# When batch 3's x is loaded, and where batch 2's scores stand, in a fused cross-attention and gated feed-forward kernel

## The chip, the cores and the metric

The kernel runs on one core of a Trainium2 chip. The core has a matrix engine (TensorE, PE in the profile), a vector engine (VectorE, DVE), a scalar engine (ScalarE, ACT), a general engine (GpSimd, POOL) and a synchronising engine (SyncE, SP), which here only issues transfers. Each engine runs its own list of instructions in order. Transfers are carried by 16 DMA engines, which all queues share. The metric is the device time of the launch in microseconds (us); lower is better. Four runs of the kernel before took 228.4 to 231.78 us, median 230.49.

## The reference

There are B = 8 batches with H = 8 heads, S = 512 tokens, Ns = 32 state rows and D = 64 values a head. For each batch and head the tokens read the state by a softmax over the 32 state rows, and the state rows read the tokens by a softmax over the 512 tokens. Both results stand one after the other and go through a gated feed-forward layer.

```python
scores  = scale * x @ state.T;   a  = softmax(scores);  xread = a  @ state
scores2 = scale * state @ x.T;   a2 = softmax(scores2); sread = a2 @ x
y   = concatenate([xread, sread], axis=2)        # B, H, S + Ns, D
t   = y.transpose(0, 2, 1, 3).reshape(B * (S + Ns), H * D)
out = (sigmoid(t @ w_gate) * (t @ w_val)) @ w_out     # 512 -> 1536 -> 512
```

## The kernel before

**Tiling.** A batch's 512 tokens are four chunks of 128 (index `c`), its eight heads two halves of four (index `i`), the 1536 hidden columns twelve groups of 128 (index `f`, NF = 12). Arithmetic on TensorE is in bf16.

**A batch's stages.** `load_x` (L70) brings x from memory in fp32 as one transfer of 1 MB; the caller names the queue, SP or GpSimd. `cast_x` (L100) makes it bf16 (`xb`). `at_xT_dma` (L125) has SP issue four DMA transposes, one a chunk, which give `xT`. `S_mm` (L130) computes the scores of one half of the heads with eight matmuls; every group of four matmuls needs all four chunks of `xT`. `S_exp` (L136, ScalarE) makes E; `n_sum` (L150) and `n_mul` (L171, VectorE) make the normalised `ab`; `aT_dma` (L194) has SP issue four DMA transposes of it, which give `aT`. `at_Eb` (L142, GpSimd) makes a bf16 copy of E, which the matmuls of the state read (`sr_mm`, L203) use.

**Feed-forward.** The state is multiplied into the gate and value weights first (`sw_mm`, L234; `sw_wide`, L257, is half of a batch's share), which gives `SW`. `gv_mm` (L282) multiplies `SW` by `aT`, four matmuls a group; `gv_th` (ScalarE) and `gv_glu` (VectorE) make the gated product; `out_mm` (L312) multiplies a third of the groups of one chunk by `wo`, four matmuls a call, and every third call finishes a chunk, which ScalarE scales and SP writes out.

**Order.** No scheduler: the order of the source is the order on every engine. Batches 0 and 1 have a start-up written out by hand (L393 to L582), which does all their gate/value work. Then a loop over b from 1 to 8 and over f from 0 to 11 (L584) interleaves the output of batch b - 1, the gate/value work of batch b and the attention of batch b + 1 (`nb`). For b = 1 there is no gate/value work left, and f = 0, 1, 2 only call `out_mm` for batch 0; the scores of batch 2 follow the second of these calls. The state weights of batch 2 (`sw_wide`) come at f = 3 and 6, its state read at f = 9, its first gate/value group at b = 2, f = 0, and the scores of batch 3 at b = 2, f = 1 and 2.

**Around the change.** On GpSimd's queue the transfers of the start-up stand in this order: the last weight loads, x of batch 2 (L504), three loads of `wo` (L505 to L507, 512 KB each), x of batch 3 (L508). GpSimd then pads a state tile (L576) and casts x of batch 2 and of batch 3 as each lands. SP issues the four transposes of batch 2's `xT`, the four of batch 3's, then the four of batch 2's `aT`, then the output writes. The tiles `xb`, `xT`, `aT`, `ab` and E have two buffers each, x in fp32 has three, the output tiles have four. `gate` (L85) is a one-element copy on GpSimd whose only purpose is that GpSimd's queue waits until its argument has landed; it is used in the start-up already:

```python
    def gate(landed):
        nc.gpsimd.tensor_copy(pre[:, 1:2], landed)
```

Of the kernel before, what the change touches and what calls it, by code (L numbers as in the profile page):

```python
# [16 lines left out]
def kernel(  # L17
# [14 lines left out]
    nc = tc.nc  # L32
# [31 lines left out]
    AT, OU, GV, SWP = (p_at, "at"), (p_out, "outp"), (p_gv, "gv"), (p_sw, "swp")  # L64
    xfs, xbs, xTs = {}, {}, {}
# [4 lines left out]
    def load_x(b, eng, parts=1, hold=None):  # L70
        xf = stg.tile((128, H, 4, D), FP, name="xf")
        if hold is not None:

            hold.memset(xf[:, 0, 0, 0:1], 0.0)
        v = x[b].rearrange("h (p c) d -> p h c d", c=4)
        n = H // parts
        for i in range(parts):
            eng.dma_start(xf[:, n * i:n * i + n], v[:, n * i:n * i + n])
        xfs[b] = xf
# [5 lines left out]
    def gate(landed):  # L85

        nc.gpsimd.tensor_copy(pre[:, 1:2], landed)
# [8 lines left out]
    def load_wo(q):  # L96
        nc.gpsimd.dma_start(wo[:, 4 * q:4 * q + 4],
                            moe_w_out.rearrange("(k p) n -> p k n", p=128)[:, 4 * q:4 * q + 4])

    def cast_x(b, cp, lo, n):  # L100
        if b not in xbs:
            xbs[b] = xp.tile((128, 4, H, D), BF, name="xb")
        cp(xbs[b].rearrange("p c h d -> p h c d")[:, lo:lo + n], xfs[b][:, lo:lo + n])  # L103


    def xT_tile(b):
        if b not in xTs:
            xTs[b] = ap_.tile((128, 4, 4, 128), BF, name="xT")
        return xTs[b]
# [15 lines left out]
    def at_xT_dma(b):  # L125
        xT = xT_tile(b)
        for c in range(4):
            nc.sync.dma_start_transpose(xT[:, :, c], xbs[b][:, c].rearrange("p h d -> p (h d)"))  # L128

    def S_mm(b, i, place):  # L130
        ps = held["S", b, i] = place[0].tile((128, 4, 2, 2, Ns), FP, name="Sp", tag=place[1])
        for jj in range(2):
            for c in range(4):
                nc.tensor.matmul(ps[:, c, :, jj], xTs[b][:, 2 * i + jj, c], sTz[:, b, 2 * i + jj], start=True, stop=True)  # L134

    def S_exp(b, i):  # L136
        if b not in E1s:
            E1s[b] = ap_.tile((128, 4, 2, 4, Ns), FP, name="E1")
        nc.scalar.activation(E1s[b][:, :, :, 2 * i:2 * i + 2].rearrange("p c e j n -> p (c e) j n"),  # L139
                             held["S", b, i].rearrange("p c e j n -> p (c e) j n"), AF.Exp, scale=scale)  # L140
# [6 lines left out]
    def halfE(b, i):  # L147
        return E1s[b][:, :, :, 2 * i:2 * i + 2].rearrange("p c e j n -> p (c e) j n")

    def n_sum(b, i):  # L150
        rs = ap_.tile((128, 8, 2), FP, name="rs")
        nc.vector.tensor_reduce(rs, halfE(b, i), AX.X, ALU.add)  # L152
        ri = held["ri", b, i] = ap_.tile((128, 8, 2), FP, name="ri")
        nc.vector.reciprocal(ri, rs)
# [16 lines left out]
    def n_mul(b, i, eng):  # L171
        if b not in abs_:
            abs_[b] = ap_.tile((128, 4, 2, 128), BF, name="ab")
        ri = held["ri", b, i]
        eng.tensor_tensor(abs_[b].rearrange("p c e (j n) -> p (c e) j n", n=Ns)[:, :, 2 * i:2 * i + 2], halfE(b, i),  # L175
                          ri.unsqueeze(3).to_broadcast((128, 8, 2, Ns)), ALU.mult)
# [7 lines left out]
    def aT_tile(b):  # L184
        if b not in aTs:
            aTs[b] = ap_.tile((128, 4, 2, 128), BF, name="aT")
        return aTs[b]
# [6 lines left out]
    def aT_dma(b):  # L194
        for c in range(4):
            nc.sync.dma_start_transpose(aT_tile(b)[:, c], abs_[b][:, c].rearrange("p e k -> p (e k)"))  # L196
# [60 lines left out]
    def sw_wide(b, v):  # L257

        if b not in SWs:
            SWs[b] = fp.tile((128, 2, 2, dff), BF, name="SW", bufs=2)  # L260
        lo = 768 * v
        for k, places in enumerate(((OU, AT), (SWP, SWP), (SWP, SWP))):
            pss = [p[0].tile((128, 512), FP, name="swp", tag=p[1]) for p in places]
            if k < 2:
                sw_mm(pss, b, k, lo, 512, 0)
            else:
                for w in range(2):
                    sw_mm(pss, b, w, lo + 512, 256, 256 * w)
            for e in range(2):
                if k < 2:  # L270
                    sw_left[b, v, k, e] = (SWs[b][:, e, k, lo:lo + 512], pss[e])
                else:
                    sw_left[b, v, k, e] = (SWs[b][:, e, :, lo + 512:lo + 768], pss[e].rearrange("p (w n) -> p w n", w=2))

    def sw_cp(b, lo, w, e, cp):
        cp(*sw_left.pop((b, lo, w, e)))  # L276
# [5 lines left out]
    def gv_mm(b, f, place):  # L282
        n = n_of(b)
        fs = slice(f * 128, (f + 1) * 128)
        pss = []
        for w in range(2):
            ps = place[0].tile((128, 512), FP, name="gvp", tag=place[1])[:, :n]
            if b < B:
                for g in range(2):
                    nc.tensor.matmul(ps, SWs[b][:, g, w, fs], aTs[b][:, :, g], start=(g == 0), stop=(g == 1))  # L290
            else:
                for j in range(4):
                    nc.tensor.matmul(ps, (wg, wv)[w][:, j, fs], XS[:, j], start=(j == 0), stop=(j == 3))  # L293
            pss.append(ps)
        held["gv", b, f] = pss
# [209 lines left out]
    load_wo(0)  # L505
    load_wo(1)
    load_wo(2)  # L507
    load_x(3, nc.gpsimd)  # L508
    sw_cp(1, 512, 0, 1, act)
    gv_mm(0, 6, SWP)  # L510
    gv_glu(1, 1)
# [64 lines left out]
    pad(2, 6)  # L576
    cast_x(2, pool, 0, 4)
    cast_x(2, pool, 4, 4)
    cast_x(3, pool, 0, 4)
    cast_x(3, pool, 4, 4)  # L580
    at_xT_dma(2)
    at_xT_dma(3)  # L582

    for b in range(1, B + 1):  # L584
        nb = b + 1 if b + 1 < B else None
        for f in range(NF):

            v, q = divmod(f, 6) if b > 1 else (0, f - 3) if f < 6 else (1, f - 6)
            if nb is not None and q == 0:
                sw_wide(nb, v)  # L590
                sw_cp(nb, v, 0, 0, act)
                sw_cp(nb, v, 0, 1, act)
            ahead = nb is not None and q == 0
            for first in (ahead, not ahead):
                if first and b > 1:
                    gv_mm(b, f, SWP if b == B and f % 2 else GV)
                    gv_th(b, f)
                    gv_glu(b, f)
                elif not first and (b < B or f < 9):
                    out_mm(b - 1, f)  # L600
            if nb is not None:
                if q == 0:
                    sw_cp(nb, v, 1, 0, vec)
                if b == 1 and f == 1:
                    for i in range(2):
                        S_mm(nb, i, (AT, OU)[i])
                        S_exp(nb, i)
                        n_sum(nb, i)
                        n_mul(nb, i, nc.vector)
                    aT_dma(nb)  # L610
                for k in ({1: (3,), 3: (4,), 4: (5,)} if b > 1 else {0: (3,), 1: (4, 5)}).get(q, ()):
                    sw_cp(nb, v, k // 2, k % 2, act)
                g = f
                if g in (1, 2) and b > 1:
                    S_mm(nb, g - 1, AT)
                    S_exp(nb, g - 1)
                if f in (6, 7):
                    n_tok(nb, f - 6)
                    if f == 7:
                        n_split(nb, 0)  # L620
                elif f == 8:
                    n_split(nb, 1)
                elif f == 9:
                    sr_mm(nb, AT)
                    sr_inv(nb)
                    if b == 1:
                        sr_fin(nb)
                elif f == 10 and b > 1:
                    sr_fin(nb)
                if g in (2, 4) and b > 1:  # L630
                    n_sum(nb, g // 2 - 1)
                elif g in (3, 5) and b > 1:
                    n_mul(nb, g // 2 - 1, nc.vector)
                if g == 3:
                    at_Eb(nb)
                if nb + 2 < B and f == (6 if b == 1 else 3):
                    load_x(nb + 2, nc.sync)
                if g == 5 and b > 1:
                    aT_dma(nb)
                if f == 5 and b > 1:  # L640
                    if nb + 1 < B:
                        cast_x(nb + 1, pool, 0, 4)
                        cast_x(nb + 1, pool, 4, 4)
                        at_xT_dma(nb + 1)
# [33 lines left out]
```

## Time and profile before

| What | Value |
|---|---|
| median of four runs | 230.49 us |
| lowest and highest | 228.4 and 231.78 us |
| the profiled execution's own time | 230.5 us |
| its span, first to last instruction | 228.7 us |
| granted TensorE clock | 1.000 |
| bytes moved by DMA | 27.57 MB |
| transposes `xT`: issues, median issue to landing | 24, 2.5 us |
| transposes `aT`: issues, median issue to landing | 24, 2.4 us |
| loads of x from SP, 1 MB: median issue to landing | 7.0 us |
| loads of x from GpSimd, 1 MB (batches 2 and 3): median | 14.6 us |
| loads of `wo` from GpSimd, 512 KB: median | 12.6 us |

Times in the profile are microseconds from the first instruction. A row of the chain or of a timeline gives the start, the length, the engine with the line of the source, and what is written from what is read; "q" after an engine's name is its sequencer, which issues transfers; a trailing bracket gives the idle time before the row and what ended it. The row of slices shows forty equal parts of the span, 5.7 us each, with the busy share in tenths. q0 is the queue of the transfers that GpSimd issues, q1 the one of those that SP issues.

### The profile page before, as it was taken

Reading aid. Unit: us, or ns where it says so; the run is one execution under the profiler, and the core shown is the slowest. Engines: PE = TensorE matmul, PEld = TensorE weight load, DVE = VectorE, ACT = ScalarE, POOL = GpSimd, SP = SyncE. Lnnn points to the kernel's source line nnn. Section 1 sums busy time; section 2 is a strip of 40 time slices with the busy share of each in tenths; the row PEclk is TensorE's granted clock in tenths of the full one; section 3 lists DMA queues with packets and bytes.
Section 4 is the critical chain, followed back from the end, with each engine's and each line's share of the span. In section 5 each row is a group of like instructions: output and inputs, shape, how many; then the busy total and the mean of one; then the engine's idle time right before and its main releaser. Section 6 shows DMA issues by size and latency. Waiting matters only on the chain.

```text
span 228.7 us, 4786 instructions
## 1 busy us (share of the span) xinstructions
PE 218.1 (95%) x1855; PEld 113.1 (49%) x1880; DVE 139.9 (61%) x233; ACT 130.7 (57%) x244; POOL 46.0 (20%) x90
## 2 busy tenths in 40 slices
PE   7779999979999999999999999999999999999994
PEld 6655345434444445444444544454445444466744
DVE  2489899838358854886488747874687443332311
ACT  3569787548458476756675567556755544422411
POOL 2897930060015000600060006000200000000001
PEclk9999999999999999999999999999999999999999
DMA  6899999953499243824373431234122111112104
GB/s 218 244 202 187 215 260 254 123 90 79 113 289 236 68 96 112 250 52 79 117 230 84 82 118 46 69 72 138 46 71 70 47 49 46 47 64 77 46 23 115
DMA packets 37990, 27.57 MB, mean 121 GB/s; under 512 B 20976, under 2 KB 33136, under 8 KB 37968
## 3 DMA queue, kind: packets, MB, share of 16 engines
q1 hardware_dynamic: 31408, 20.26, 34.2%
q0 software_dynamic: 6416, 6.95, 16.5%
q8 instruction: 14, 0.23, 0.4%
q14 instruction: 8, 0.07, 0.1%
q10 hardware_dynamic: 144, 0.07, 0.1%
HBM read 18.35 MB, written 8.91 MB: 119 GB/s over the span
## 4 chain that ended last, share of the span: by engine, by line
PE 73%; DMA 15%; POOL 4%; SPq 3%; ACT 2%; issue 1%; DVE 0%; POOLq 0%; ACTq 0%
PE outp L321 33%; PE gvp L290 28%; PE gvp L293 5%; DMA xf<-in_x_dram 4%; DMA xT<-xb 4%; PE swp L238 4%; DMA wg<-in_moe_w_gate_dram 3%; DMA sf<-in_state_dram 2%; SPq L128 2%; DMA aT<-ab 2%; SPq L196 1%; PE Sp L134 1%; PE outp L341 1%; POOL xb L103 1%; PE srp L215 1%
## 5 line engine op out<-in xcount | busy, mean ns | idle before, releaser
L305 DVE SCALAR_TENSOR_TENSOR glu<-th,gvp 128x512 bf16<-128x512 f32 (+1 forms) x108 | 70.4, 657 | 63.4 <-ACT th L300 47.7
L290 PE MATMUL gvp<-aT,SW 128*128 128x512 bf16 x384 | 96.4, 379 | 0.4 <-DMA aT<-ab 0.3
L321 PE MATMUL outp<-wo,glu 128*128 128x512 bf16 x371 | 95.1, 379 | 1.3 <-issue 0.2
L300 ACT ACTIVATE th<-gvp 128x512 f32<-128x512 f32 (+1 forms) x108 | 61.5, 575 | 60.3 <-PE gvp L290 50.3
L290 PEld LDWEIGHTS <-SW 128*128 128x128 bf16 x384 | 36.1, 98 | 45.7 <-issue 5.1
L321 PEld LDWEIGHTS <-glu 128*128 128x128 bf16 x396 | 37.4, 98 | 40.8 <-issue 0.4
L276 ACT CAST SW<-swp 128x512 bf16<-128x512 f32 x76 | 42.0, 590 | 3.9 <-PE swp L238 2.6
L145 POOL CAST Eb<-E 128x256 bf16<-128x256 f32 x32 | 12.0, 415 | 96.7 <-ACT E L139 96.7
L325 ACT ACTIVATE res<-outp 128x512 f32<-128x512 f32 x33 | 19.8, 599 | 17.1 <-PE outp L321 17.1
L103 POOL CAST xb<-xf 128x1024 bf16<-128x1024 f32 (+1 forms) x14 | 15.9, 1157 | 16.1 <-DMA xf<-in_x_dram 16.1
L276 DVE CAST SW<-swp 128x512 bf16<-128x512 f32 x20 | 13.6, 685 | 0.8 <-PE swp L238 0.7
L152 DVE TENSOR_REDUCE rs<-E 128x16 f32<-128x512 f32 x16 | 10.9, 680 | 4.8 <-ACT E L139 4.7
L332 POOL DMA_DIRECT2D out_dram<-res x2 | 1.0, 528 | 60.0 <-ACT res L325 60.0
L139 ACT ACTIVATE E<-Sp 128x512 f32<-128x512 f32 x16 | 9.6, 604 | 6.1 <-PE Sp L134 6.0
L175 DVE TENSOR_TENSOR ab<-E,ri 128x512 bf16<-128x512 f32 x15 | 12.9, 864 | 0.1
L160 DVE TENSOR_REDUCE E<-E 128x128 f32<-128x512 f32 x12 | 12.3, 1035 | 0.0
L238 PE MATMUL swp<-wg,sTc 64*32 64x256 bf16 (+1 forms) x256 | 11.5, 329 | 0.6 <-DMA wg<-in_moe_w_gate_dram 0.3
L238 PEld LDWEIGHTS <-sTc 64*32 64x32 bf16 x512 | 6.4, 90 | 10.5 <-issue 7.5
L238 PE MATMUL swp<-wv,sTc 64*32 64x256 bf16 (+1 forms) x256 | 10.4, 323 | 0.0
L220 DVE RECIPROCAL r<-srp 128x128 f32<-128x128 f32 x8 | 7.6, 952 | 1.5 <-PE srp L215 1.5
L134 PE MATMUL Sp<-sTz,xT 128*128 128x64 bf16 x128 | 6.7, 193 | 1.9 <-DMA xT<-xb 1.1
L355 PE MATMUL warm<-ident 128*128 128x128 bf16 x80 | 7.2, 266 | 1.4 <-POOL ident masks.py:199 1.4
(54 smaller groups left out, 110.5 us busy)
## 6 DMA issues: line engine op xcount, KB each, us to landing
out_dram<-res SPq DMA_DIRECT2D x31, 256.0 KB, 2.5
xf<-in_x_dram SPq DMA_DIRECT2D x5, 1024.0 KB, 7.0
xf<-in_x_dram POOLq DMA_DIRECT2D x2, 1024.0 KB, 14.6
wo<-in_moe_w_out_dram POOLq DMA_DIRECT2D x3, 512.0 KB, 12.6
xf<-in_x_dram SPq DMA_DIRECT2D x2, 512.0 KB, 5.9
wg<-in_moe_w_gate_dram POOLq DMA_DIRECT2D x2, 512.0 KB, 7.5
wv<-in_moe_w_val_dram POOLq DMA_DIRECT2D x2, 512.0 KB, 6.6
sf<-in_state_dram SPq DMA_DIRECT2D x1, 512.0 KB, 4.5
```

Of the source, the lines that this page charges most:

```text
L103: cp(xbs[b].rearrange("p c h d -> p h c d")[:, lo:lo + n], xfs[b][:, lo:lo + n])
L145: nc.gpsimd.tensor_copy(Ebs[b][:, c], E1s[b][:, c])
L160: nc.vector.tensor_reduce(held["E4", b][:, e].rearrange("p j n -> p (j n)"), E1s[b][:, :, e].rearrange("p c j n -> p (j n) c"), AX.X, ALU.add)
L175: eng.tensor_tensor(abs_[b].rearrange("p c e (j n) -> p (c e) j n", n=Ns)[:, :, 2 * i:2 * i + 2], halfE(b, i), ri.unsqueeze(3).to_broadcas ...
L238: nc.tensor.matmul(pss[e][j * Ns:(j + 1) * Ns, o:o + n], sTc[rows, b, j], (wg, wv)[w][rows, j, lo:lo + n], start=True, stop=True)
L276: cp(*sw_left.pop((b, lo, w, e)))
L290: nc.tensor.matmul(ps, SWs[b][:, g, w, fs], aTs[b][:, :, g], start=(g == 0), stop=(g == 1))
L293: nc.tensor.matmul(ps, (wg, wv)[w][:, j, fs], XS[:, j], start=(j == 0), stop=(j == 3))
L300: nc.scalar.activation(th, held["gv", b, f][0], AF.Tanh, scale=0.5)
L305: nc.vector.scalar_tensor_tensor(glus[b][:, f], held["th", b, f], 1.0, held["gv", b, f][1], ALU.add, ALU.mult)
L321: nc.tensor.matmul(ops[b, c], glus[b][:, f, c * 128:(c + 1) * 128], wo[:, f], start=(f == 0), stop=(f == NF - 1))
L325: nc.scalar.activation(res, ops[b, c], AF.Copy, scale=0.5)
```

## The change

It has two parts. The load of x of batch 3 leaves its place behind the `wo` loads; it now stands behind the casts of batch 2, after a `gate` on an element of chunk 3 of batch 2's `xT`, so GpSimd issues it when the fourth transpose has landed. The transposes of batch 3's `xT` leave the start-up. The block of batch 2's scores, their sums and products and its `aT` transposes moves from after the second output group of batch 0 to before the first; the transposes of batch 3's `xT` now follow that block. On SP's queue, batch 2's `aT` so stands ahead of batch 3's `xT`. On TensorE sixteen score matmuls stand ahead of eight output matmuls that they followed. The order on VectorE and ScalarE stays. No other transfer or operation is added but the gate's one-element copy.

```diff
     load_wo(0)
     load_wo(1)
     load_wo(2)
-    load_x(3, nc.gpsimd)
     sw_cp(1, 512, 0, 1, act)
...
     cast_x(2, pool, 0, 4)
     cast_x(2, pool, 4, 4)
+    at_xT_dma(2)
+    gate(xTs[2][:, 0, 3, 0:1])
+    load_x(3, nc.gpsimd)
     cast_x(3, pool, 0, 4)
     cast_x(3, pool, 4, 4)
-    at_xT_dma(2)
-    at_xT_dma(3)
...
                 sw_wide(nb, v)
                 sw_cp(nb, v, 0, 0, act)
                 sw_cp(nb, v, 0, 1, act)
+            if b == 1 and f == 0:
+                for i in range(2):
+                    S_mm(nb, i, (AT, OU)[i])
+                    S_exp(nb, i)
+                    n_sum(nb, i)
+                    n_mul(nb, i, nc.vector)
+                aT_dma(nb)
+                at_xT_dma(3)
             ahead = nb is not None and q == 0
...
                 if q == 0:
                     sw_cp(nb, v, 1, 0, vec)
-                if b == 1 and f == 1:
-                    for i in range(2):
-                        S_mm(nb, i, (AT, OU)[i])
-                        S_exp(nb, i)
-                        n_sum(nb, i)
-                        n_mul(nb, i, nc.vector)
-                    aT_dma(nb)
```

## The prediction

> **What bounds the kernel now.** I read the page first (busy shares, slices, chain by line), then the chain in order of time from 20 to 66 us, then TensorE's timeline where that chain leaves TensorE, and last what the DMA queues did just before.
>
> The page: busy time of each engine, then the slices.
>
> ```profile
> PE 218.1 (95%) x1855; PEld 113.1 (49%) x1880; DVE 139.9 (61%) x233; ACT 130.7 (57%) x244; POOL 46.0 (20%) x90
> PE   7779999979999999999999999999999999999994
> POOL 2897930060015000600060006000200000000001
> PEclk9999999999999999999999999999999999999999
> DMA  6899999953499243824373431234122111112104
> ```
>
> TensorE is the bound, at the full granted clock. After the start-up its only slice under nine tenths is the ninth (45.7 to 51.5 us). There the chain leaves TensorE:
>
> ```profile
> 32.84 2.03 POOL xb L103 x2
> 34.89 1.28 SPq L128
> 36.22 1.42 SPq L128
> 37.68 1.35 SPq L128
> 39.07 9.02 DMA xT<-xb
> ...
> 57.65 3.69 DMA aT<-ab
> 61.34 0.14 issue
> 61.48 1.02 PE gvp L290 x4
> ```
>
> The four transposes of x of batch 2 are issued from 34.89 and the last lands at 39.07 + 9.02 = 48.09. From 61.48 to the end the chain is TensorE with hardly a break, so time won before 61.48 is won at the end. TensorE alone, same place:
>
> ```profile
> 44.41 1.89 PE L321 MATMUL outp<-wo,glu 128*128 128x512 bf16 x7
> 46.66 0.55 PE L134 MATMUL Sp<-sTz,xT 128*128 128x64 bf16 x2 [0.36 <-DMA xT<-xb]
> 47.50 0.20 PE L134 MATMUL Sp<-sTz,xT 128*128 128x64 bf16 x1 [0.29 <-DMA xT<-xb]
> 48.13 0.55 PE L134 MATMUL Sp<-sTz,xT 128*128 128x64 bf16 x13 [0.43 <-DMA xT<-xb]
> 48.52 1.03 PE L321 MATMUL outp<-wo,glu 128*128 128x512 bf16 x4
> ```
>
> Two output groups of batch 0 (eight matmuls) run, then the score matmuls trickle in as transposes land. And this is what the queues moved between 34.9 and 38.6 us, and between 42.5 and 46.4 us (packets, MB, share of the 16 engines; two views, one fence each):
>
> ```profile
> q0 software_dynamic: 740, 0.81, 122.9%
> ```
>
> ```profile
> q1 hardware_dynamic: 561, 0.13, 123.8%
> q0 software_dynamic: 26, 0.09, 7.1%
> ```
>
> In the first stretch the transposes (queue q1) have been issued and move no packet: q0, with wo and x of batch 3 queued on it, has all engines. In the second only 26 packets of q0 are left, yet q1 crawls at 0.13 MB in 3.9 us. From 46.4 to 48.1 the same view gives q1 970 packets and 0.23 MB. x of batch 3 is issued at 26.47 with 20.0 us to landing, so at 46.5: the transposes run freely once its last packets are gone.
>
> **Part 1: x of batch 3 leaves the queue.** Still ahead of the transposes are the three wo loads, the last issued at 25.74 and landed 16.8 later (the longest of line 97), at 42.5. Freed, the first transpose of before landed at about 46.6 (34.89 plus the longest landing time, 11.7) and the last at 48.1, so the four come in within 1.5 of each other, 1.6 after x3. From 42.5 instead of 46.5 that is about 44.1. Bounds: unhindered transposes need 6.4 from first issue to last landing (batch 3: issued from 48.62, aT issue follows at 53.85, landings 2.5 after issue), which gives 41.3; if x3 was not what held them, 48.1. I take 44.1, the nearest row being the same transposes after the same kind of release.
>
> [...] The trace row is q1 with no packet for 3.7 us beside a full q0. [...] By the row they stand behind what was queued earlier, and removing it brings 4 us. [...]
>
> **Part 2: scores ahead of all output of batch 0.** The sixteen score matmuls pass the eight output matmuls, so their start is due when the gate/value matmuls end, 44.4 instead of 46.1. With the transposes in at 44.1 there is no wait. What goes: from the end of the eight output matmuls (last start 45.92, one every 0.215, so 46.13) to the next output at 48.52 are 2.39 us; undisturbed, eight score matmuls push the output by 0.23 (112.20 to 112.43), sixteen by 0.46. Saved 1.93. The moved rows carry two exponentials (0.60 each) on ScalarE, and two sums, two reciprocals and two products (0.68, 0.25 and 0.7 each) on VectorE. Their order on both engines is unchanged, so they only start earlier: ScalarE's last tanh ends at 44.78, VectorE's last glu at 45.50. In before the first exponential starts at 48.55 and the last product ends at 52.59, 4.04 later; now 44.85 and 48.9.
>
> Batch 2's aT transposes move past xT of batch 3 on SP's queue. They were issued from 53.85, landed at 61.34, and TensorE waited: the weight matmuls at 60.32 to the first gate/value at 61.48 took 1.16, against 0.78 in the next batch (72.46 to 73.24). Issued at 48.9, they land near 56; due at 59.5. Saved 0.38. Sum 2.31.
>
> **Part 3: what waits longer.** GpSimd now holds at the gate until the fourth transpose has landed (one element copied, 0.19), then issues x3 (0.94, as before), and behind it stand the two casts of x3 and the four Eb casts of batch 2. [...] Landing: 44.4 + 7.0 = 51.4; the nearest load from GpSimd (x2) took 9.3 with weight loads ahead of it, which gives 53.7; I take 51.4, as nothing is ahead. Casts 2.03 make 53.4, Eb 1.9 makes 55.3. Batch 2's state read needs Eb at 58.04 - 1.93 = 56.1. Cover 0.8. Then SP: aT of batch 2 from 48.9 and xT of batch 3 behind it. Eight such transposes took 48.62 to 61.34, 12.7, in before, so all lie in SBUF by 61.7 (by casts at 53.4 plus 6.4: 59.8). Batch 3's scores need them at 64.93 - 2.31 = 62.6. Cover 0.9. Behind those, SP's output writes and the load of x of batch 4 go out at about the old times (60.3 and 61.35); the output tiles have four buffers and the fifth is not written before about 67 us, and x4, landing at 68.4, may hold its cast (69.36, now 67.1) by 1.3, which the 5 us between that cast and the SP slot at 74.11 take up. Casts beside a product slow it: 1.17 against 0.68 at 117.12. If x3 lands during the products, aT is 0.5 later, inside its 3.5 us of cover. All this is priced at nothing, with covers of under 1 us in two places.
>
> **Sum.** The profiled run took 230.5 for a span of 228.7; the median of the four is 230.49, the same. 230.5 - 2.3 = 228.2, or 1.0% less. The aim lies on the 1% line, which is about what a measurement of this kernel can tell from no change.
>
> **Rivals.**
> - The transposes come in between: wo's tail, or the crawl itself, holds them until 45 to 46.5, or x3 lands at 52.1 to 54 and Eb costs some of the saving. Each us late costs one: 228.9 to 230.4. For it: wo's last landing was 42.5 though its neighbour took only 12.6 (37.6), so that tail is uncertain.
> - The cover is gone (slower). If the landing stays where it was, TensorE sits at the head of the scores from 44.4 to 48.1 with nothing before it; the 1.73 us (eight matmuls by 0.215) that hid part of the wait now come after it. Price +1.73 - 0.38 = +1.35, 231.8. It decides from a landing at about 46.7 (44.4 plus the saving); over 1% slower from 49. [...] Against: the release at 46.5 coincides with x3's landing.
> - GpSimd's queue becomes the bound (slower). Eb of batch 2 stands behind x3's casts. Break-even is x3 landing at 54.4, over 1% slower at 56.7; if x3 took the 14.6 us that is the median of the two GpSimd loads, it lands at 59.0, the state read waits 6.9, and the time is 228.2 + 6.9 = 235. Against: those two had up to 2.5 MB queued ahead, x3 now has none.
>
> **Chances.** Forecast 0.64 (own range 227.5 to 228.9; 0.38 of it better than 1%, 0.26 not; I lean to the better side because earlier scores also relieve VectorE's cast at 52.51); in between 0.16, all within 1%; cover gone 0.13, of which 0.08 slower than 1%; GpSimd's queue 0.07, of which 0.05. Faster 0.38, same 0.49, slower 0.13. The range 227.4 to 231.3 leaves out about 0.13 above and 0.05 below.
>
> **What would show it.** Right: all transposes of xT of batch 2 landed by 44.5, no wait of the scores for xT, the first output of batch 0 at about 44.9, the first gate/value of batch 2 at about 59.2 with no wait for aT, x3 landing near 51. Wrong: a wait for xT ahead of the first score above 1 us, state-read matmuls waiting for Eb, or scores of batch 3 waiting for xT at 62 us. The forecast falls if wo alone holds the transposes, or if x3's load on a quiet queue is much slower than 7 us.

## The result, and the profile after

The changed kernel took 229.07 us, median of 40 runs (227.09 to 233.63), against 230.73 us for the kernel before (61 runs, 228.4 to 235.39). The ratio is 0.9931, 95% interval 0.9912 to 0.995: 0.5 to 0.9% faster, which is clear of the noise, but under the 1% that I had aimed at. The forecast was 228.2, range 227.4 to 231.3. The ratio leaves out the runs that lie more than 1.5% above the fastest of their kernel. The profiled execution took 227.62 us for a span of 225.7, 3.0 less than in the profile before. That is more than the change brings; the table below shows why.

Two of the same rows of the page after:

```profile
PE   7679999999999999999999999999999999999994
PEclk9999999999999999999999999999999999999999
```

The dip in TensorE's ninth slice is gone. The chain there now runs through TensorE and ScalarE's casts of the state weights, with no DMA from 44 us on (its longer rows; a piece of 0.65 at 49.07 has no name in the profile):

```profile
44.05 0.47 PE Sp L134 x16
...
44.78 2.32 PE outp L321 x10
47.10 0.41 PE swp L238 x8
47.52 1.55 ACT SW L276 x3
...
50.34 0.97 ACT SW L276 x2
...
51.36 0.41 PE swp L238 x15
```

Sixteen score matmuls take 0.47, as in later batches (0.23 for eight, 112.20 to 112.43 in the profile before), and no wait stands before them. Before, the same place held 2.39 us. GpSimd's timeline after:

```profile
42.80 0.19 POOL L87 CAST pre<-xT 128x1 f32<-128x1 bf16 x1 [8.87 <-DMA xT<-xb]
43.03 0.92 POOL L78 DMA_DIRECT2D xf<-in_x_dram  x1
50.73 2.03 POOL L103 CAST xb<-xf 128x1024 bf16<-128x1024 f32 x2 [6.79 <-DMA xf<-in_x_dram]
52.71 1.44 POOL L145 CAST Eb<-E 128x256 bf16<-128x256 f32 x4
```

The gate opens at 42.80: the last transpose of batch 2 landed at 42.74, 5.3 us earlier than before (48.08). x of batch 3 is issued at 43.03 and cast from 50.73; the Eb casts behind it end at 54.2, 1.2 ahead of the state-read matmuls that use them (55.39).

**Where the time went, in three stretches.** One span compares badly with another here, because the start-up varies. I therefore cut each profile at the starts of two matmuls of line 290: the last gate/value matmul of the start-up, and the first of batch 2. Microseconds; the middle stretch is the one that the change touches. The landing is counted from the first instruction, as in all rows, so it moves with the start-up.

| Profile | start-up | middle | rest | last transpose of batch 2 lands |
|---|---|---|---|---|
| before | 44.20 | 17.28 | 167.24 | 48.08 |
| before, second (e9) | 43.75 | 15.96 | 167.26 | 46.69 |
| before, third (e12) | 44.21 | 18.59 | 167.25 | 48.40 |
| after | 43.67 | 14.80 | 167.26 | 42.74 |
| after, second (e10) | 46.97 | 14.80 | 167.26 | 46.10 |
| e1, load alone | 46.12 | 15.01 | 168.82 | 45.81 |
| e2, scores alone | 43.56 | 20.07 | 167.32 | 47.44 |
| e3, no gate | 44.27 | 23.03 | 167.24 | 50.29 |
| e4, load from SP | 43.77 | 14.80 | 167.68 | 43.61 |
| e5, earlier casts | 43.93 | 14.91 | 167.26 | 44.10 |
| e6, casts and warm-up | 44.04 | 14.38 | 167.80 | 43.34 |
| e7, scores alone, wait filled | 45.69 | 17.79 | 167.25 | 47.77 |
| e8, load from SP, else before | 48.10 | 16.08 | 167.67 | 46.28 |
| e11, e4 and e5 | 46.02 | 14.38 | 167.69 | 46.01 |

The change takes the middle, which was 15.96 to 18.59 in three profiles, down to 14.80 in both profiles of it, and leaves the rest alone. It removes a wait that varied from one execution to the next: the last transpose landed 2.9 to 4.2 us after the end of the start-up before, and 0.9 ahead of it after. Against the profile that I predicted from it saves 2.48; the other 0.5 of the 3.0 is start-up.

### The profile page after: what moved, and what is told of

Same layout as the page of the kernel before. It is cut to its first block, busy times and chain, and to the rows that moved or that the text cites. A ratio compares the mean times of both kernels' runs of the same rounds, so it can differ in the third digit from the quotient of the medians.

```text
span 225.7 us, 4786 instructions
## 1 busy us (share of the span) xinstructions
PE 216.6 (96%) x1855; PEld 112.2 (50%) x1880; DVE 140.7 (62%) x233; ACT 130.6 (58%) x244; POOL 45.5 (20%) x91
## 4 chain that ended last, share of the span: by engine, by line
PE 87%; DMA 6%; POOL 2%; issue 2%; ACT 1%; another core or an unknown queue 0%; DVE 0%; POOLq 0%
PE gvp L290 37%; PE outp L321 36%; PE swp L238 5%; PE gvp L293 5%; DMA wg<-in_moe_w_gate_dram 4%; DMA sf<-in_state_dram 2%; PE srp L215 1%; PE Sp L134 1%; PE outp L341 1%; ACT SW L276 1%; PE srp L212 1%; POOL wv L83 1%; POOL pre L87 1%; POOL sTz L391 1%; POOL wg L83 0%
## 5 line engine op out<-in xcount | busy, mean ns | idle before, releaser
L325 ACT ACTIVATE res<-outp 128x512 f32<-128x512 f32 x33 | 19.7, 598 | 17.2 <-PE outp L321 16.4
L145 POOL CAST Eb<-E 128x256 bf16<-128x256 f32 x32 | 11.5, 400 | 87.6 <-ACT E L139 87.6
L103 POOL CAST xb<-xf 128x1024 bf16<-128x1024 f32 (+1 forms) x14 | 15.2, 1108 | 15.0 <-DMA xf<-in_x_dram 12.1
L175 DVE TENSOR_TENSOR ab<-E,ri 128x512 bf16<-128x512 f32 x15 | 13.6, 914 | 0.1
L134 PEld LDWEIGHTS <-xT 128*128 128x128 bf16 x128 | 5.6, 98 | 3.7 <-issue 1.1
```

The source lines that it names most:

```text
L145: nc.gpsimd.tensor_copy(Ebs[b][:, c], E1s[b][:, c])
L325: nc.scalar.activation(res, ops[b, c], AF.Copy, scale=0.5)
```

## The experiments

Each edit is against the changed kernel unless it says otherwise. Ratios are to the kernel before, run beside it.

**e1: only the load is moved.** The block of scores goes back behind the second output group, batch 3's `xT` still after batch 2's `aT`.

```diff
-            if b == 1 and f == 0:
-                for i in range(2):
-                    S_mm(nb, i, (AT, OU)[i])
...
+                if b == 1 and f == 1:
+                    for i in range(2):
+                        S_mm(nb, i, (AT, OU)[i])
...
+                    aT_dma(nb)
+                    at_xT_dma(3)
```

> Only the load of x of batch 3 is moved (behind the gate); the scores of batch 2 stay after the second output group, their aT transposes still ahead of batch 3's xT on SP. Theory (the queued load held the transposes): transposes of batch 2 land by about 43 in the profile, the scores find them there, no wait; 1.9 us of the saving is kept and most of the 0.4 at aT, so about 1.5 to 2.3 us under before; batch 3's xT may land near 63 and cost up to 0.8. Rival (the earlier place of the scores brings the time): like before, within 0.4 us.

Measured 230.4 us, ratio 0.9989 (0.9952 to 1.0026), so the time is like the rival's. The profile, though, shows the theory's half: no wait for `xT` at batch 2's scores, a middle of 15.01, 2.3 under the first profile of before. The gain is given back after it, in a rest 1.58 longer than before's. TensorE at batch 3's scores:

```profile
65.34 0.32 PE L134 MATMUL Sp<-sTz,xT 128*128 128x64 bf16 x5 [0.50 <-DMA xT<-xb]
...
67.22 0.40 PE L134 MATMUL Sp<-sTz,xT 128*128 128x64 bf16 x8
68.36 1.02 PE L321 MATMUL outp<-wo,glu 128*128 128x512 bf16 x4 [0.74 <-ACT res L325]
```

and SP's queue just before:

```profile
52.63 5.04 SPq L196 DMA_TRANSPOSE aT<-ab  x4
57.77 6.28 SPq L128 DMA_TRANSPOSE xT<-xb  x4
64.15 1.00 SPq L327 DMA_DIRECT2D out_dram<-res  x2
```

Batch 3's transposes now end so late that its scores wait (0.50), and the writes of batch 0's finished outputs, queued behind them on SP, go out 3 us after the first gate/value matmul of batch 2 (64.15 against 61.13; in the changed kernel 59.94 against 58.47, 1.5 after). TensorE then waits 0.74 for ScalarE's scaling of the next output. ScalarE was itself held by the four output tiles, of which the first was still being written: that write landed at 67.61 and the scaling began at 67.71. The row of e1 names another releaser, but in e6, where the same scaling waits, the row names the write:

```profile
63.98 0.60 ACT L325 ACTIVATE res<-outp 128x512 f32<-128x512 f32 x1 [0.76 <-DMA out_dram<-res]
```

So moving the load removes the wait, and moving the scores starts SP's work early enough not to pay for it.

**e2: only the scores are moved.** The load is back behind `wo`, with no gate.

```diff
     load_wo(2)
+    load_x(3, nc.gpsimd)
...
-    gate(xTs[2][:, 0, 3, 0:1])
-    load_x(3, nc.gpsimd)
```

> Only the scores move ahead of all output of batch 0 and SP's order changes; the load of x of batch 3 stays behind the wo loads. Theory: the transposes land late as before (46 to 48 us), TensorE waits about 3 us ahead of the scores with nothing to cover it; 0.5 to 1.4 us slower than before. Rival (the place of the scores brings the time): 1.5 us or more faster than before.

Measured 233.91 us, ratio 1.014 (1.0069 to 1.0211). The direction is the theory's, the size about double. TensorE:

```profile
45.97 0.20 PE L134 MATMUL Sp<-sTz,xT 128*128 128x64 bf16 x1 [2.03 <-DMA xT<-xb]
46.39 0.20 PE L134 MATMUL Sp<-sTz,xT 128*128 128x64 bf16 x1 [0.21 <-DMA xT<-xb]
46.86 0.20 PE L134 MATMUL Sp<-sTz,xT 128*128 128x64 bf16 x1 [0.27 <-DMA xT<-xb]
47.48 0.88 PE L134 MATMUL Sp<-sTz,xT 128*128 128x64 bf16 x13 [0.42 <-DMA xT<-xb]
48.17 4.10 PE L321 MATMUL outp<-wo,glu 128*128 128x512 bf16 x12
```

The same twelve output matmuls take 2.75 in the changed kernel. Stretches of 2 us of e2 give the reason (length; then busy time and instructions of PE, PEld, DVE, ACT, POOL; the granted clock; DMA share, GB/s):

```profile
46.00:48.00 2.00, 1.10 (x13) 0.78 (x14) 0.00 (x0) 0.00 (x0) 1.23 (x2) 0.87 0.45 75
48.00:50.00 2.00, 2.00 (x12) 0.90 (x10) 1.21 (x3) 1.09 (x2) 0.82 (x3) 0.50 0.04 8
50.00:52.00 2.00, 2.00 (x9) 0.71 (x7) 1.93 (x4) 0.00 (x0) 1.07 (x2) 0.77 0.00 0
```

TensorE's clock is at half from 47.49, for 3.41 us. Half a clock for 3.41 loses up to 1.7 (an estimate, for a TensorE that is busy throughout), on top of the bare wait. Ahead of the fall TensorE was idle for 2.9 us here, with single matmuls in between, and for 1.5 in the third profile of before (0.61, 0.18, 0.29 and 0.44 in the four rows of its scores), which also lost its clock for 3.41 us from 49.47; the first profile waited 1.08 and kept it.

**e3: no gate.** x of batch 3 is issued as soon as batch 2 is cast.

```diff
     at_xT_dma(2)
-    gate(xTs[2][:, 0, 3, 0:1])
     load_x(3, nc.gpsimd)
```

> The changed kernel without the gate: GpSimd issues the load of x of batch 3 as soon as batch 2 is cast (about 34 us), beside the transposes. Theory (what is queued on the 16 engines first goes first): the two streams meet, the last transpose lands 1 to 3 us later than the 42.7 of the changed kernel, so up to 2 us slower than it. Rival (only the 20 us in the queue behind wo mattered): same as the changed kernel within 0.3 us.

Measured 235.29 us, ratio 1.0215 (1.0159 to 1.027), 6 us above the changed kernel and beyond what the theory allowed. GpSimd issued the load at 35.39 and SP the first transpose at 35.47; they met from the start. The load landed 12.9 later, the last transpose at 50.29, and TensorE stood idle (first row of the scores), with the clock at half for 6.8 us after:

```profile
49.09 0.50 PE L134 MATMUL Sp<-sTz,xT 128*128 128x64 bf16 x2 [4.44 <-DMA xT<-xb]
```

So on GpSimd's queue the wait that the change adds is what makes it work. A later place in the queue without it is worse than before.

**e4: the load on SP's queue, behind the transposes, and no gate.**

```diff
     at_xT_dma(2)
-    gate(xTs[2][:, 0, 3, 0:1])
-    load_x(3, nc.gpsimd)
+    load_x(3, nc.sync)
```

> The changed kernel with the load of x of batch 3 on SP's queue right behind the four transposes of batch 2, and no gate. Theory: transposes are ahead of it in the same queue, they land by about 43; x of batch 3 lands near 47 instead of 50.6; time as the changed kernel within 0.3 us, since its slack was covered. Rival (the time of batch 3's x bounds something): faster than the changed kernel by 0.5 us or more.

Measured 229.01 us, ratio 0.9946 (0.9905 to 0.9987): like the changed kernel. x of batch 3 landed at 46.69, 3.9 us earlier, and the middle is 14.80 again. The earlier landing gains nothing, and in the same queue behind the transposes the load needs no gate.

**e5: earlier casts.** ScalarE casts two state-weight tiles of batch 2 one step earlier, in the first half ahead of the first output scaling. The edit does the same in the second half, which the expectation does not mention.

```diff
-... else {0: (3,), 1: (4, 5)}).get(q, ()):
+... else {0: (3, 4, 5)}).get(q, ()):
```

> The changed kernel, but ScalarE casts the last two state-weight tiles of batch 2's first half right after the first three, ahead of the first output scaling instead of behind it. In the changed kernel TensorE's second state-weight group waits for those casts (0.71 instead of 0.29 us in one row of eight). Theory: 0.3 to 0.5 us faster than the changed kernel. Rival (that row is no wait): same within 0.2 us.

Measured 227.83 us over 6 runs, ratio 0.9896 (0.9853 to 0.994), whose interval overlaps that of the changed kernel. None of the six lost its clock; against the executions of the changed kernel that kept theirs (median 228.16) it is 0.3 less. The row that took 0.71 takes 0.29, so it was a wait. The 0.4 was lost again in this profile, since x of batch 3 landed late (52.03) and the state read now waited for Eb behind its casts:

```profile
55.85 0.54 PE L215 MATMUL srp<-Eb,xb 128*128 128x64 bf16 x13 [0.15 <-POOL Eb L145]
```

This is the second half of the rival "in between", in which Eb costs some of the saving from a landing at 52.1 on; here it landed at 52.03.

**e6: e5 with 16 more warm-up matmuls in the start-up.**

```diff
+    warm(16, OU)
     cast_x(1, act, 4, 4)
```

> As e5_casts, with 16 more warm-up matmuls (1.0 us) in the start-up, ahead of the transposes of x of batch 1, where TensorE waits 1.1 to 2.7 us for a cast. Theory (a wait of about 2.7 us there costs a 3.4 us stretch at half clock in part of the executions): fewer executions with a granted clock of 0.993 or less, median 0.5 to 1.5 us under e5_casts. Rival (the clock falls for another reason): same share, same time or up to 1 us slower.

Measured 229.01 us, ratio 0.9925 (0.9886 to 0.9964). It missed: 4 of 12 executions still had a granted clock of 0.993 or less, against 16 of 41 of the changed kernel and none of 6 of e5, and the median is above e5's. Its rest is 0.54 longer, from the wait for the output tile shown under e1.

The profiles do show where the start-up varies. The five of fourteen with a start-up over 45.6 us, and no other, had half a clock in it, for 3.41 us (6.83 in e8), between 15.1 and 21.9 us. In four of the five TensorE waited 2.45 to 3.31 us at that point for ScalarE's cast of x of batch 1, whose load had landed at 13.76 to 14.68 us; in the other ten profiles it landed by 12.91 and the wait was at most 1.49. The second profile of the changed kernel is one of the four (a row of TensorE, and two stretches, columns as under e2):

```profile
15.80 1.07 PE L118 MATMUL xTp<-ident,xb 128*128 128x128 bf16 x16 [3.27 <-ACT xb L103]
```

```profile
16.00:18.00 2.00, 2.00 (x44) 1.69 (x42) 0.69 (x1) 1.50 (x2) 2.00 (x6) 0.84 1.28 198
18.00:20.00 2.00, 2.00 (x40) 1.50 (x38) 1.59 (x3) 1.52 (x3) 0.21 (x1) 0.50 1.02 130
```

All of it lies ahead of the first thing that the change moves, x of batch 3, which before was issued at 26.47. So the long start-ups of these profiles are not the change's doing. Why that early load sometimes lands late stays open.

**e7: e2 with its wait filled by 48 idle-filling matmuls.**

```diff
             if b == 1 and f == 0:
+                warm(48, AT)
                 for i in range(2):
```

> As e2_scores_only, with 48 idle-filling matmuls (about 3 us at full clock) ahead of the scores, where TensorE waited. Theory (e2's loss of some 3 us is the bare wait plus a 3.4 us stretch at half clock that the wait brought on): full clock after it, and 1 to 2 us faster than e2_scores_only though it does more work; that is 1 to 2 us slower than before. Rival (the loss is the wait alone): as e2_scores_only or slower.

The time is inconclusive: 233.53 us over 4 runs, ratio 1.0131 (1.0062 to 1.02), beside e2's 1.014. The middle is 17.79 against 20.07, though it holds 2.84 us of added matmuls, but that comparison is not clean: the profiled start-up was 2.1 longer, so most of the wait for the transposes was over when it ended (the last landed 2.1 us after it, against 3.9 in e2). What the profile shows is that behind the filled wait the twelve output matmuls take 2.75 again instead of 4.10, as at the full clock of the changed kernel; whether this execution would have lost its clock without the filling is not shown:

```profile
45.90 2.84 PE L355 MATMUL warm<-ident 128*128 128x128 bf16 x48
48.90 0.63 PE L134 MATMUL Sp<-sTz,xT 128*128 128x64 bf16 x16
49.36 2.75 PE L321 MATMUL outp<-wo,glu 128*128 128x512 bf16 x12
```

**e8: before, with the load on SP behind the transposes.** Against before, whose scores and SP order stay:

```diff
-    load_x(3, nc.gpsimd)
...
     at_xT_dma(2)
+    load_x(3, nc.sync)
     cast_x(3, pool, 0, 4)
     cast_x(3, pool, 4, 4)
     at_xT_dma(3)
```

> Before, with one thing changed: x of batch 3 is loaded from SP's queue right behind the transposes of batch 2; the scores stay after the second output group and SP's order stays (xT of batch 3, then aT of batch 2). Theory (the load queued ahead is what cost the time, the scores' place only matters where batch 3's x comes late): no wait for xT at the scores, 1.5 to 2 us under before; aT may still be waited for, 0.4 us. Rival (the scores have to move too): like e1_load_only, within 0.5 us of before.

Measured 232.78 us, ratio 1.0056 (1.0012 to 1.0101). The rival is nearer: nothing is gained. The time is even above before, by 0.1 to 1.0%, where the rival allowed 0.2%. The scores wait for nothing, but x of batch 3 lands at 49.59, its transposes are issued from 51.77 and stand ahead of `aT`, which TensorE then waits for:

```profile
64.18 1.04 PE L290 MATMUL gvp<-aT,SW 128*128 128x512 bf16 x4 [1.01 <-DMA aT<-ab]
```

**e9, e10, e12: both kernels profiled again, unchanged.**

> The kernel before, profiled a second time, to see how far the wait for the transposes of batch 2 repeats. If the profiled execution was typical: last transpose of batch 2 at 47 to 49 us, 2.4 us between the eight output matmuls and the next, as there. If it was an extreme one: landing a microsecond or more earlier, and a loss of 1.5 us or less.

> The changed kernel, profiled a second time. Theory: again no wait for xT at the scores and none for aT; x of batch 3 lands within 2 us of 50.6. If the first profile was lucky, a wait shows at the scores or at the state read's Eb.

> The kernel before, profiled a third time, for the same question as e9_before_again and with the same two outcomes.

The table has them. Before: middle 15.96 and 18.59 around the first profile's 17.28, so the wait is there each time and spread over 2.6 us, of which the half clock of the third explains up to 1.7. After: 14.80 again, with no wait for `xT` or `aT`, though its start-up was 3.3 us longer; x of batch 3 landed at 52.47.

**e11: e4 and e5 together.**

```diff
+    load_x(3, nc.sync)
...
+... else {0: (3, 4, 5)}).get(q, ()):
```

> The changed kernel with the earlier casts of e5_casts and the load of x of batch 3 on SP as in e4_x3_on_sp. In e5_casts the state read waited 0.2 us for Eb behind a late x of batch 3, which lands 4 us earlier from SP. Theory: that wait goes, so within 0.3 us of e5_casts or better, 2 to 3 us under before. Rival (SP's load in front of aT takes that back): 0.5 us or more above e5_casts.

Measured 230.27 us, ratio 0.9943 (0.9904 to 0.9982). The state read no longer waits for Eb. The middle is 14.38, 0.42 under the changed kernel, and the rest 0.43 longer, all of it behind the last matmul, as in every kernel whose load came from SP (e4, e8); why is open. In the profile that is a wash. The interval overlaps those of e5 and of the changed kernel, so neither the theory nor the rival is decided, and no version here is shown to be faster than the changed kernel.

## Why the prediction was right, and what was off

**Part 1, the landing.** The mechanism holds. In all fourteen profiles the first transpose of batch 2 lands 0.06 to 1.41 us after the last transfer that GpSimd had issued before it: 46.44 and 46.61 in the first of before, 39.50 and 39.95 after, 48.29 and 49.05 in e3. Two terms were off, and that the sum came within 1.4 us was in part luck. I kept 42.5 for the last `wo` load, which landed at 39.50: it was issued 0.7 earlier, and took 14.4 us (14.4 to 16.1 in the nine profiles without x of batch 3 issued right behind it, 15.6 to 17.2 in the five with it). And I gave the four transposes 1.6 us behind that landing; they took 3.24, to 42.74. The error cost nothing, since the scores were not due before.

**The order of the two queues.** From one row of before, q1 with no packet for 3.7 us beside a full q0, I took it that transposes stand behind what was queued earlier. After, between 37 and 38 us, both queues move in the same microsecond:

```profile
q0 software_dynamic: 138, 0.13, 77.9%
q1 hardware_dynamic: 365, 0.09, 51.3%
```

In the two microseconds ahead of these q1 moved nothing, as before. But my two stretches of before left out the one between them, from 38.6 to 42.5 us, with x of batch 3 and the last of `wo` under way:

```profile
q0 software_dynamic: 260, 0.89, 78.0%
q1 hardware_dynamic: 645, 0.16, 37.4%
```

There the transposes did share. So the profiles show neither sharing from the start (no packet of q1 for 3.7 us) nor a strict "behind": what holds in all fourteen profiles is that no transpose of batch 2 is complete before the last load that GpSimd issued ahead of it. Why q1 then crawls beside 26 packets of q0, and what happens on one single DMA engine, no view here shows.

**Part 2, the scores.** The sum for the middle was right (2.31 said, 2.48 measured against that profile), its split was not. I booked the 1.93 on the earlier place of the scores. e1 shows the wait gone with the scores where they were; their earlier place is worth the 1.56 by which e1's rest is longer than that of the changed kernel. The 0.38 at `aT` went as forecast: `aT` landed at 54.75, the first gate/value matmul of batch 2 came 0.79 after its weight matmuls began.

**Part 3, the covers.** x of batch 3 was forecast at 51.4, 7.0 after an issue at 44.4; it was issued at 43.03 and landed at 50.61, 7.6 later; batch 3's `xT` at 61.7 and landed at 61.07; both covers held. That they are thin shows where they break: in e5 with a landing of x 1.4 us later, and in e1 with transposes of batch 3 that land 4.2 us after the first gate/value matmul of batch 2 instead of 2.6.

**From 228.2 to 229.07.** The step that was off is the last: I took the four runs' median and one profile as one and the same point. That profile's wait was longer than a typical one. Its span is 228.7. Of 63 executions of before, run beside the experiments, 32 kept the full clock, with a median span of 227.9; e9, with a middle of 15.96, has 227.0. The executions at full clock have a median time of 229.79 before and 228.16 after (25 of 41), 1.63 apart, and the medians of all runs differ by 1.66, where my sum said 2.31. So the term that was too large is the wait, read off one profile. That the changed kernel's median is 229.07 and not 228.16 comes from the executions that lost some of their clock, as many do in both kernels. The middles of single profiles differ by 1.16 to 3.79; the 2.48 that fits my 2.31 belongs to that one profile.

**The rivals.** "The cover is gone" is e2: right in its mechanism, too small in price. It had 1.35 for the wait and nothing for the clock that fell with the wait there, up to 1.7; together 3.0, and the ratio of e2 makes 3.2. "In between" did not occur in the two profiles of the changed kernel; e5 shows its beginning. "GpSimd's queue" did not come: x of batch 3 landed 6.1 and 7.6 us after its issue, where that rival feared up to 14.6.

## What to carry to other kernels

A transfer that was not needed yet held up a later one that was, on another queue: with x of batch 3 issued 8.4 us ahead of batch 2's transposes the last of them landed at 48.08, with x of batch 3 issued behind them at 42.74. So look for what was issued ahead of a late landing, and make the unneeded load wait for it. Only putting it later was not enough: without the gate (e3) the last transpose landed at 50.29 and the kernel took 235.29 us. When work is freed on the bound engine, follow the next queue in order (here SP's): in e1 the output writes behind it went out 3.0 us after the first gate/value matmul of batch 2, against 1.5 in the changed kernel, and a rest 1.58 longer took the gain back. Price a wait of two or three microseconds on TensorE with the clock that it may cost, not with its length alone: in e2, 2.9 us of idle time were followed by 3.41 us at half the clock. And before a wait read from one profile is booked as a saving, take the profile again: here it came out between 1.2 and 3.8 us.

## What the runs showed of the hardware that I had not expected

In e3 a load of x beside the transposes delayed them far more than they delayed it. Both were issued behind `wo`, whose last load landed at 41.0; the load of x landed 7.3 us after that, about what it took alone in the changed kernel (7.6), and the last transpose 9.3 after it, where without the load it took 3.2 (42.74 against 39.50).

And TensorE lost half its clock over short waits. All six profiles with a single wait of 2.03 us or more (the longest 4.44) lost it, for 3.41 or 6.83 us. Two of the fourteen lost it after less: the third of before after 1.52 us of idle time in four pieces, and one in its start-up, where the wait for the cast of x of batch 1 was at most 1.49. In nine others that wait was at most 1.49 too, and their start-ups had no half clock; the first profile of before kept its clock after 1.08 us in three pieces at the scores. What decides between these no run shows.
